# Folding the values of grouped heads into the first weights: eight 64x32 tiles per chunk in two banks instead of pairs of 128x64 tiles per half chunk

## The chip, the cores and the metric

The kernel runs on one core of a Trainium2 chip. The metric is the device time of one execution in microseconds (us); lower is better. A timing is the median of several runs.

## What is computed

Three stages follow each other. An attention over 32 memory slots per head reduces keys and values to 32 rows per head; a dense layer with a leaky activation and then a sum over four gated experts follow. Cut to what matters:

```python
# 4 batches, 8 heads, 576 tokens, head size 64, 32 memory slots
a = exp(phi - max(phi, axis=2)); a = a / (sum(a, axis=2) + 1e-9)
k_m = einsum('bhsm,bhsd->bhmd', a, k)
v_m = einsum('bhsm,bhsd->bhmd', a, v)
scores = q @ k_m.T / sqrt(64)
attn = softmax(scores)                       # 576 x 32 per head
x = concat_over_heads(attn @ v_m)            # 2304 x 512
h = x @ w_in                                 # w_in 512 x 2048
g = max(h, 0) + alpha * min(h, 0)
y = g @ w_out                                # w_out 2048 x 512
p = probs / (sum(probs) + 1e-9)
out = sum over e of p[:, e] * (max(y @ w1[e], 0) @ w2[e])   # 4 experts, 512 -> 1024 -> 512
```

## The kernel before

The product `attn @ v_m @ w_in` isn't formed in that order. For each batch b and each chunk c of 512 of the 2048 columns of `w_in`, the kernel first multiplies the 32 x 64 values of each head into the 64 rows of `w_in` that belong to that head. This is the **fold** (`fold`, line 519). Its result is a 256 x 512 matrix, 32 rows for each of the 8 heads, and the dense layer then multiplies it by the 256 x 576 attention weights of the batch.

A fold works on half a chunk (e is 0 or 1, 256 columns) and one PSUM bank. The 8 heads are two groups g of four. A stationary operand has 128 rows (two heads of 64) and 64 columns (2 x 32 memory slots), and is zero where the rows of one head meet the columns of the other. `att_sum` (line 285) makes these zeros with a small product by a mask (line 289), and `att_memc` (line 328) with two scaled copies that use it. There are four such matmuls of 256 columns in a fold, in float32, two for each group, side by side in the two halves of the array's columns. Then `fold_hi` (line 531, on ScalarE) copies the bank to SBUF in the rounded fp32r form, and `fold_lo` (line 536, on VectorE) writes the remainder. For batch 0, chunk 0 (`plain`) there is a float32 copy alone.

`First` is a step of the dense layer: chunk c, batch b, half k of the tokens (288 of them), and 128 columns f; there are 128 steps, numbered j = 32c + 8b + 4k + f. Its tasks are `u` (`up`: six fp32r matmuls on the folded weights, four float32 instructions where plain), `n` and `v` (the two sides of the activation, ScalarE and VectorE), `h` and `l` (rounded and remaining part, ScalarE and VectorE or GpSimd), `d` (`down`: 12 matmuls into four PSUM banks that stay open over four steps) and `e` (those four banks are emptied). The experts run after these steps.

All work is issued in an order written out by hand, the string `ORDER` (line 34), where `f`, `fh` and `fl` are the three tasks of a fold. In the kernel before their digits are batch, chunk and half; `f201` is batch 2, chunk 0, second half. Every engine works through its own instructions in that order. The names `a31_mem`, `a10_ev0` and so on are tasks of the attention of a batch and a group: `mem` is the product with keys and values, `memc` copies it out of PSUM, `sc0` and `sc1` are scores of the two halves of the tokens, `ev0` and `ev1` turn them out of PSUM on VectorE.

PSUM has eight banks. Two are kept for the `u` tasks. The other six (`ps_a`, line 208) are handed out to all else, in the order in which they came free: four are held by an open group of `d` tasks, and two are left for folds and for the attention. A task whose bank isn't free yet waits for the last reader of the bank that comes free next. Folded weights have four buffers (`wpp`, line 212).

The steps of the dense layer that need folds run from about 25 to 410 us, the experts after that.

Of the kernel before, what the change touches and what calls it, by code (L numbers as in the profile page):

```python
# [21 lines left out]
HB = S // 2  # L22
# [13 lines left out]
  a01_natc a01_nath a00_natc w2 a01_nathc a01_mem in0_1 in0_0 in0_2 a00_mem a01_memc in1_1 in1_0 out0_1 in1_2 a01_memt  # L36
  a00_memc in0_3 a01_memtc a00_memt out0_0 a01_sc0 a00_memtc in1_3 a00_sc0 a01_ev0 in0_4 w3 a00_ev0 q1 s010_max p2
  s000_max kv2 s010_sub a11_max s000_sub a10_max s010_exp a11_exp s010_sum in1_4 s000_exp a11_nat a10_exp s010_mul
  s000_sum f000 s010_back a11_natc s000_mul a10_nat a11_sum fh000 a11_nath s000_back a10_natc out0_2 u0 a11_nathc
  a01_sc1 out0_3 n0 a00_sc1 a01_ev1 out0_4 in2_1 u1 q2 a00_ev1 s01288_max in3_1 in2_0 a11_mem n1 s00288_max s01288_sub  # L40
  a10_sum s00288_sub s01288_exp in2_2 s00288_exp a10_mem a11_memc in3_0 out0_5 in3_2 a11_memt a10_memc in2_3 a11_memtc
  a10_memt s00288_sum in2_4 a11_sc1 a10_memtc s01288_sum a11_sc0 s00288_mul a10_sc1 a11_ev0 a10_sc0 v0 in3_3 s00288_back
  s01288_mul a10_ev1 in3_4 s01288_back d0
# [3 lines left out]
out2_5 out3_2 out3_3 u6 in5_1 out3_4 p3 v3 f100 out3_5 v4 n5 s100_max s110_sub d3  # L47
n6 a21_max v5 s110_exp s100_sub u7 e3 v6 out1_6 s110_sum f101 s100_exp a20_max out2_6 d4
fh100 s100_sum n7 s110_mul fl100 a21_exp d5
s100_mul a20_exp out3_6 s110_back fh101 s100_back d6  # L50
pst in6_1 s01288_lo fl101 s100_hi v7 s110_hi s100_lo d7
s110_lo a20_sum s00288_lo q3 a21_sum s000_lo u8 e7 s010_lo u9 in4_0 a20_nat in4_2 n8 a21_nat n9 u10 v8 in4_3 h8 a21_nath
  a21_natc u11 l8 v9 n10 d8
in5_0 a20_natc v10 a21_nathc in5_2 u12 h9 h10 a20_mem l9 l10 n11 in5_3 n12 v11 in6_0 a21_mem a20_memc v12 h11 in4_4
  a30_max h12 a30_exp l11 a20_memt kv3 l12 d9
a21_memc a30_sum in5_4 a20_memtc a31_max in7_1 a21_memt in6_2 a31_exp a20_sc0 u13 a20_ev0 a21_memtc a31_sum a20_sc1 n13
  in6_3 a21_sc1 out4_1 a20_ev1 in6_4 u14 a21_ev1 s200_max a21_sc0 n14 d10
s200_sub a21_ev0 s210_max a31_nat s210_sub s200_exp a30_nat v13 a31_natc d11
s200_sum s210_exp a30_natc s210_sum s200_mul a31_nath e11 f200 s210_mul u15 a31_nathc v14 d12
h13 s200_back h14 l13 s210_back fh200 l14 a31_mem n15 fl200 s200_hi v15 s210_hi s200_lo a30_mem a31_memc s210_lo h15  # L60
  in7_0 out5_1 l15 in7_2 a31_memt a30_memc u16 out4_0 a31_memtc u17 n16 out4_2 a30_memt n17 a31_sc0 v16 a30_memtc d13
v17 h16 a31_ev0 l16 in7_3 a30_sc1 h17 a30_sc0 l17 a30_ev1 a31_sc1 a30_ev0 in7_4 f201 s300_max a31_ev1 s300_sub d14
fh201 s310_max fl201 s300_exp d15
s310_sub out6_1 s300_sum s310_exp u18 e15 s310_sum s300_mul u19 f300 s310_mul n18 d16
s300_back n19 v18 s300_hi v19 u20 h18 s310_back s300_lo h19 d17
s310_hi l18 fh300 l19 u21 n20 s310_lo d18
n21 v20 fl300 h20 u22 l20 v21 d19
out4_3 h21 n22 l21 out4_4 u23 e19 v22 u24 out5_0 out6_0 f301 out5_2 h22 n23 d20
l22 fh301 v23 n24 fl301 d21
h23 v24 out4_5 l23 out5_3 h24 u25 l24 d22  # L70
n25 out4_6 out5_4 out7_1 v25 u26 out5_5 out6_2 h25 u27 n26 d23
l25 n27 v26 out6_3 h26 u28 e23 l26 u29 v27 out6_4 f010 out5_6 h27 n28 d24
l27 out7_0 n29 v28 d25
v29 h28 fh010 l28 out6_5 fl010 d26
h29 out7_2 in8_1 l29 u30 out7_3 d27
n30 out6_6 in9_1 v30 u31 out7_4 e27 in8_0 u32 in8_2 f011 h30 n31 l30 d28
in9_0 n32 v31 in9_2 h31 d29
fh011 l31 out7_5 v32 u33 out7_6 h32 d30
n33 l32 fl011 in10_1 v33 u34 in8_3 h33 d31
l33 n34 in9_3 v34 u35 e31 in10_0 u36 in10_2 f110 n36 in10_3 d32  # L80
h34 v36 fh110 l34 in8_4 n35 fl110 d33
h36 v35 in11_1 l36 u37 h35 in9_4 u38 l35 n37 in11_0 d34
n38 v37 in11_2 h37 out8_1 d35
l37 v38 out8_0 h38 u39 e35 in10_4 u40 n39 l38 f111 out9_1 v39 n40 d36
out8_2 h39 fh111 v40 d37
l39 h40 fl111 l40 u41 in11_3 d38
n41 out8_3 in11_4 v41 u42 out8_4 h41 d39
n42 l41 out9_0 out8_5 v42 u43 e39 out8_6 h42 u44 n43 l42 f210 out10_1 v43 n44 u45 out9_2 h43 d40
fh210 l43 v44 n45 fl210 d41
h44 v45 out11_1 l44 out9_3 d42  # L90
h45 l45 out10_0 u46 out9_4 out10_2 u47 n46 d43
n47 v46 out10_3 h46 out9_5 u48 l46 e43 u49 out9_6 n48 f211 v47 in12_1 v48 d44
h47 out11_0 fh211 l47 out10_4 fl211 d45
# [12 lines left out]
h60 fl020 out13_1 l60 u61 in15_2 d58
n61 out12_0 out12_2 u62 v61 d59
n62 in15_3 h61 v62 u63 l61 e59 h62 u64 l62 n63 f021 n64 v63 out12_3 h63 d60
fh021 l63 v64 fl021 in15_4 d61
h64 l64 out14_1 u65 out13_0 out12_4 d62  # L110
n65 out13_2 out12_5 u66 v65 out13_3 h65 u67 n66 l65 d63
out12_6 n67 v66 v67 h66 u68 e63 h67 l66 u69 out15_1 l67 n68 f120 out14_0 n69 v68 d64
out13_4 fh120 v69 out13_5 fl120 d65
h69 out14_2 d66
h68 l69 l68 out14_3 u70 out13_6 d67
out15_0 n70 out14_4 v70 out14_5 u71 e67 h70 out14_6 u72 n71 f121 l70 v71 n72 u73 out15_2 h71 d68
fh121 l71 fl121 n73 d69
# [6 lines left out]
h77 wl00 u78 e75 u79 n78 f221 l77 v78 n79 d76
ws01 h78 fh221 d77
fl221 u80 u81 f320 l78 v79 n80 d78
h79 v80 fh320 l79 u82 h80 fl320 n81 d79
l80 v81 n82 u83 e79 h81 u84 l81 f321 n83 v82 h82 d80
v83 fh321 l82 h83 fl321 n84 l83 u85 u86 v84 n85 d81
h84 v85 l84 n86 d82  # L130
h85 v86 l85 d83
h86 l86 u87 e83 u88 n87 f030 n88 v87 h87 d84
v88 fh030 l87 fl030 d85
h88 l88 d86
d87
u89 e87 u90 n89 f031 n90 v89 h89 d88
v90 fh031 l89 h90 fl031 u91 l90 u92 n91 d89
n92 v91 h91 v92 u93 l91 h92 u94 l92 n93 d90
n94 v93 h93 v94 d91
l93 h94 l94 u95 e91 u96 n95 f130 n96 v95 h95 d92  # L140
v96 fh130 l95 fl130 d93
h96 l96 u97 u98 n97 d94
n98 v97 h97 v98 u99 l97 h98 d95
l98 n99 v99 u100 e95 h99 u101 l99 n100 f131 n101 v100 d96
v101 fh131 fl131 d97
h100 l100 d98
h101 l101 u102 u103 n102 d99
n103 v102 h102 v103 u104 l102 e99 h103 u105 l103 n104 f230 n105 v104 d100
fh230 v105 fl230 d101
h105 l105 d102  # L150
h104 l104 u106 u107 n106 d103
n107 v106 h106 v107 u108 l106 h107 e103 u109 l107 n108 f231 n109 v108 d104
v109 fh231 x0t0 x0h0 fl231 d105
# [38 lines left out]
def memory_attention_experts(ctx: ExitStack, tc: tile.TileContext, phi, q, kv, w_in, w_out, w1, w2, alpha, dp, out):  # L192
# [42 lines left out]
    mask = const.tile([128, 2], F32, name="mask")  # L235
# [1125 lines left out]
```

## Time and profile before

| | |
|---|---|
| median of 3 runs | 1166.19 us (1165.74 to 1166.47) |
| span of the profiled execution, first to last instruction | 1164.3 us |
| TensorE (PE) busy, share of the span | 1142.6 us, 98% |
| VectorE (DVE) | 853.2 us, 73% |
| ScalarE (ACT) | 473.1 us, 41% |
| GpSimd (POOL) | 410.0 us, 35% |
| mean granted TensorE clock | 0.994 of 2.4 GHz |

The profile gives no time of the profiled execution beside its span; the median of the runs lies 1.9 us above the span. Busy time of TensorE is the time in which at least one matmul is under way, and matmuls overlap, so its cost is read from starts: from the start of one group of matmuls to the start of the next. PEld are the loads of stationary operands. A row of a timeline says start, length, engine, line, operation, what is written and read, shapes, count, and in brackets the idle time ahead of it and who ended it. One matmul call on float32 operands makes two instructions, and one on fp32r makes one.

### The profile page before, as it was taken

The page shows a single profiled execution, that of the slowest core. Times are in us where ns is not written, and L with a number is a line of the kernel's source. Part 1 is how long each engine was busy: PE and PEld are TensorE (multiplying, and loading weights), DVE is VectorE, ACT ScalarE, POOL GpSimd, SP SyncE. Part 2 cuts the span into 40 slices and gives each one's busy share as a digit, 9 for nine tenths or more (in the row PEclk, how much of TensorE's full clock was granted, in tenths as well). Part 3 has the DMA queues.
Part 4 walks back from the last instruction along what each step waited for, and adds up shares of the span by engine and source line. Part 5 has one row for each costly group of instructions (what it writes and reads, how often), then busy time and mean ns, then how long its engine had stood idle before and what let it go on. Part 6 is the DMA issues. An engine that isn't in the chain of part 4 may idle for free.

```text
span 1164.3 us, 21801 instructions
## 1 busy us (share of the span) xinstructions
PE 1142.6 (98%) x8628; PEld 1096.0 (94%) x8628; DVE 853.2 (73%) x1573; ACT 473.1 (41%) x1035; POOL 410.0 (35%) x333
## 2 busy tenths in 40 slices
PE   8899999999999989999999999999999999999998
PEld 7578999999999989999999999999999999999998
DVE  6999888885558674767757766678667777777794
ACT  5567756555455534333323333223432222222220
POOL 2333022322010164745646456433333333333320
PEclk9999999999999989999999999999999999999999
DMA  9740221312000262745637455485545556555512
GB/s 375 274 177 20 73 91 55 91 37 82 1 1 1 85 258 104 279 169 212 242 120 296 152 220 227 172 303 197 181 158 189 164 165 185 162 181 182 163 65 72
DMA packets 64214, 180.02 MB, mean 155 GB/s; under 512 B 6640, under 2 KB 23024, under 8 KB 60400
## 3 DMA queue, kind: packets, MB, share of 16 engines
q1 hardware_dynamic: 64112, 178.63, 43.9%
q8 instruction: 68, 1.11, 0.4%
q14 instruction: 34, 0.28, 0.1%
HBM read 114.34 MB, written 64.26 MB: 153 GB/s over the span
## 4 chain that ended last, share of the span: by engine, by line
PE 88%; DVE 7%; DMA 2%; issue 2%; POOL 1%; ACT 1%; SPq 0%; DVEq 0%; ACTq 0%; POOLq 0%
PE o L914 18%; PE y L600 17%; PE c L978 13%; PE uy L806 12%; PE h L562 8%; PE ux L806 8%; PE uw L806 8%; PE pw L523 2%; DMA rawin<-in_w_in 2%; DVE g L232 1%; PE pm L325 0%; POOL g L232 0%; POOL w L232 0%; DVE h L884 0%; DVE g L581 0%
## 5 line engine op out<-in xcount | busy, mean ns | idle before, releaser
L914 PE MATMUL o<-g,w 128*128 128x288 f32 x1536 | 226.0, 296 | 0.7 <-DVE g L232 0.4
L914 PEld LDWEIGHTS o<-g,w 128*128 128x128 f32 x1536 | 211.6, 189 | 1.1 <-DVE g L232 0.6
L600 PE MATMUL y<-g,wout 128*128 128x288 f32 x1440 | 205.5, 297 | 0.0
L600 PEld LDWEIGHTS y<-g,wout 128*128 128x128 f32 x1440 | 194.2, 188 | 10.5 <-issue 7.0
L806 PE MATMUL uy<-x,w 128*128 128x288 f32 x1152 | 186.0, 297 | 3.4 <-DVE v L840 3.4
L806 PEld LDWEIGHTS uy<-x,w 128*128 128x128 f32 x1152 | 163.9, 189 | 6.0 <-DVE v L840 5.9
L978 PE MATMUL c<-gc,w2c 128*128 128x288 f32 x1008 | 156.3, 295 | 0.5 <-ACT acc L991 0.5
L978 PEld LDWEIGHTS c<-gc,w2c 128*128 128x128 f32 x1008 | 141.1, 188 | 1.0 <-ACT acc L991 1.0
L232 POOL TENSOR_TENSOR gc<-h,gc 128x576 fp32r<-128x576 f32 x56 | 83.0, 1490 | 143.0 <-ACT gc L965 99.9
L806 PE MATMUL ux<-x,w 128*128 128x288 f32 x768 | 122.8, 295 | 2.8 <-ACT v L844 2.7
L806 PE MATMUL uw<-x,w 128*128 128x288 f32 x768 | 122.7, 295 | 0.0
L806 PEld LDWEIGHTS ux<-x,w 128*128 128x128 f32 x768 | 108.6, 188 | 3.2 <-ACT v L844 3.2
L965 ACT CAST gc<-h 128x576 fp32r<-128x576 f32 x70 | 47.3, 675 | 152.0 <-DVE h L957 138.6
L562 PE MATMUL h<-a,wp 128*128 128x288 f32 x720 | 108.8, 296 | 0.1
L806 PEld LDWEIGHTS uw<-x,w 128*128 128x128 f32 x768 | 108.8, 188 | 0.0
L232 POOL TENSOR_TENSOR w<-raww,w 128x512 fp32r<-128x512 f32 (+1 forms) x48 | 76.3, 1606 | 86.6 <-ACT w L705 59.8
L562 PEld LDWEIGHTS h<-a,wp 128*128 128x128 f32 x720 | 99.5, 188 | 2.7 <-issue 1.3
L931 DVE TENSOR_TENSOR acc<-o,acc 128x288 f32<-128x288 f32 x112 | 50.8, 454 | 69.2 <-PE o L914 69.2
L581 DVE SCALAR_TENSOR_TENSOR pos<-neg,nal,pos 128x288 f32<-128x288 f32 x120 | 64.8, 544 | 43.0 <-ACT pos L576 42.5
L840 DVE TENSOR_TENSOR v<-uy,v 128x288 f32<-128x288 f32 x128 | 58.1, 454 | 50.7 <-PE uy L806 50.6
L575 ACT ACTIVATE neg<-h 128x288 f32<-128x288 f32 x128 | 53.0, 414 | 83.3 <-PE h L562 78.6
L232 POOL TENSOR_TENSOR g<-pos,g 128x288 fp32r<-128x288 f32 x29 | 24.4, 845 | 173.0 <-ACT g L585 142.8
(163 smaller groups left out, 1670.9 us busy)
## 6 DMA issues: line engine op xcount, KB each, us to landing
kw<-w SPq DMA_DIRECT2D x16, 1792.0 KB, 6.9
raww<-in_w SPq DMA_DIRECT2D x32, 512.0 KB, 3.9
w<-kw SPq DMA_DIRECT2D x32, 512.0 KB, 4.6
kS<-S SPq DMA_DIRECT2D x56, 256.0 KB, 5.0
w2c<-kS SPq DMA_DIRECT2D x28, 512.0 KB, 3.6
kw<-w SPq DMA_DIRECT2D x25, 512.0 KB, 2.7
w<-kw SPq DMA_DIRECT2D x48, 256.0 KB, 3.9
kv<-in_kv SPq DMA_DIRECT2D x8, 1152.0 KB, 12.6
```

The lines of the kernel that those rows point to most:

```text
L232: eng.tensor_tensor(out=out, in0=in0, in1=in1.bitcast(F32), op=ALU.subtract)
L523: mm(p[64 * j:64 * j + 64, g * 256:(g + 1) * 256], vt_t[b, g][:, j, :], win_t[c][:, 2 * g + j, e * 256:(e + 1) * 256], start=True, stop=True,)
L562: mm(p, wp_t[b, c, f // 2][:, x, o2 + g * 256:o2 + g * 256 + 128], a_t[b][:, y, g, o:o + HB], start=(n == 0), stop=(n == 5))
L575: nc.scalar.activation(out=neg, in_=p, func=AF.Relu, scale=-1.0)
L581: nc.vector.scalar_tensor_tensor(out=pos, in0=neg, scalar=nal[:, ft:ft + 1], in1=pos, op0=ALU.mult, op1=ALU.add)
L600: mm(First.acc[d], w[:, x, d * 128:(d + 1) * 128], self.gt[:, y, 0:HB], start=(self.start and n == 0), stop=(self.stop and n == 2))
L806: mm(p, w[:, x, a, k], operand(self.b, i)[:, y, k], start=(start and n == 0), stop=(n == 5), skip_group_check=not start)
L840: nc.vector.tensor_tensor(out=out, in0=x, in1=y, op=ALU.add)
L914: mm(self.p, w[:, x, i, d % 2 * 128:(d % 2 + 1) * 128], g, start=(m == 0), stop=(m == 11), skip_group_check=len(hps) == 1)
L931: nc.vector.tensor_tensor(out=a, in0=self.p, in1=a, op=ALU.add)
L965: nc.scalar.copy(out=t[:, 0], in_=self.raw[q])
L978: mm(self.p, w[:, x, i, m * 128:(m + 1) * 128], self.g_t[q][:, y, i], start=(k == 0), stop=(k == 5))
```

## The change

Group u now holds the four heads of parity u (0, 2, 4, 6 or 1, 3, 5, 7); the host lays out `phi`, `k` and `v` to fit, and `q` stays as it was. `att_memc` writes the product twice side by side, in one instruction, with a scale for each row, so the mask and its product are gone. After the transposition, rows 0 to 63 and 64 to 127 of `kt` and `vt` both hold keys or values, and group u uses rows 64u to 64u + 63. Scores take four 64x32 tiles for each group and half instead of two of 128x64.

A fold takes a whole chunk: eight matmuls of 512 columns, one for each head, each on a 64x32 tile of the array (row half u, column quarter t), into two banks, one for each u. For batch 0, chunk 0 it takes half a chunk, eight matmuls of 256 columns, also into two banks. `fh` and `fl` then come once for each u. In `ORDER` the fold of a whole chunk and its `fh` and `fl` stand where those of the first half stood, and the places of the second half are empty. Nothing else in `ORDER` moves.

```diff
     def att_sum(b, g):
-        nc.vector.tensor_scalar(out=mr, in0=mask, scalar1=sm, scalar2=None, op0=ALU.mult)
     def att_memc(b, g):
-        for u in range(2):
-            nc.scalar.activation(
-                out=kvb[:, :, u, :],
-                in_=p[:, 0:128].rearrange("p (t d) -> p t d", t=2),
-                func=AF.Copy,
-                scale=stats[b, g][1][:, u:u + 1],
-            )
+        nc.scalar.activation(
+            out=kvb,
+            in_=p[:, 0:128].rearrange("p (t u d) -> p t u d", t=2, u=1).to_broadcast([128, 2, 2, D]),
+            func=AF.Copy,
+            scale=stats[b, g][0],
+        )
     def att_score(b, g, hf):
-        for j in range(2):
-            o = (hf * 4 + 2 * g + j) * HB
-            mm(p[64 * j:64 * j + 64, 0:HB], kt[:, j, :], q_t[b][:, o:o + HB], start=True, stop=True)
+        r = slice(64 * g, 64 * g + 64)
+        for t in range(4):
+            o = (hf * 4 + t) * HB
+            mm(p[32 * t:32 * t + 32, 0:HB], kt[r, 32 * t:32 * t + 32], q_t[b][r, o:o + HB], start=True, stop=True)
-    def fold(b, c, e):
-        p = pw_t[b, c, e] = bank(f"pw{b}{c}{e}")
-        for g in range(2):
-            for j in range(2):
+    def fold(b, c, cols):
+        n0, n1 = cols
+        for u in range(2):
+            pw_t[b, c, u, n0] = bank(f"pw{b}{c}{u}{n0}")
+        for t in range(4):
+            for u in range(2):
+                r = slice(64 * u, 64 * u + 64)
                 mm(
-                    p[64 * j:64 * j + 64, g * 256:(g + 1) * 256],
-                    vt_t[b, g][:, j, :],
-                    win_t[c][:, 2 * g + j, e * 256:(e + 1) * 256],
+                    pw_t[b, c, u, n0][32 * t:32 * t + 32, 0:n1 - n0],
+                    vt_t[b, u][r, 32 * t:32 * t + 32],
+                    win_t[c][r, t, n0:n1],
                     start=True,
                     stop=True,
                 )
```

A part of `ORDER`, where folds stood for batch 2 and chunk 0:

```diff
-s200_sum s210_exp a30_natc s210_sum s200_mul a31_nath e11 f200 s210_mul u15 a31_nathc v14 d12
-h13 s200_back h14 l13 s210_back fh200 l14 a31_mem n15 fl200 s200_hi v15 s210_hi s200_lo a30_mem a31_memc s210_lo h15
+s200_sum s210_exp a30_natc s210_sum s200_mul a31_nath e11 f20 s210_mul u15 a31_nathc v14 d12
+h13 s200_back h14 l13 s210_back fh200 fh201 l14 a31_mem n15 fl200 fl201 s200_hi v15 s210_hi s200_lo a30_mem a31_memc s210_lo h15
-v17 h16 a31_ev0 l16 in7_3 a30_sc1 h17 a30_sc0 l17 a30_ev1 a31_sc1 a30_ev0 in7_4 f201 s300_max a31_ev1 s300_sub d14
-fh201 s310_max fl201 s300_exp d15
+v17 h16 a31_ev0 l16 in7_3 a30_sc1 h17 a30_sc0 l17 a30_ev1 a31_sc1 a30_ev0 in7_4 s300_max a31_ev1 s300_sub d14
+s310_max s300_exp d15
```

And the part around the second fold of batch 0, chunk 0, of which only the `fh` changes:

```diff
-a11_ev1 out1_1 v1 out1_0 s000_hi f001 out1_2 s010_hi s00288_hi fh001 out1_3 s01288_hi u2 out1_4 out0_6 s110_max u3
-  out2_1 a10_ev0 n2 d1
+a11_ev1 out1_1 v1 out1_0 s000_hi f001 out1_2 s010_hi s00288_hi fh0010 fh0011 out1_3 s01288_hi u2 out1_4 out0_6 s110_max u3
+out2_1 a10_ev0 n2 d1
```

## Rows read from the trace of the kernel before

**Rows 1.** Windows by stage; an engine's columns are busy us and instructions
```profile
core 0: us, PE busy (x) PEld busy (x) DVE busy (x) ACT busy (x) POOL busy (x), PEclk, DMA share, GB/s
30.00:80.00 50.00, 43.33 (x326) 31.57 (x318) 48.53 (x88) 30.27 (x79) 17.48 (x15) 0.97 0.57 208
80.00:100.00 20.00, 19.57 (x199) 15.27 (x200) 19.27 (x42) 16.06 (x46) 5.53 (x5) 1.00 0.32 121
100.00:250.00 150.00, 149.90 (x1116) 138.68 (x1114) 129.29 (x257) 91.30 (x232) 31.64 (x29) 1.00 0.23 71
250.00:372.00 122.00, 122.00 (x909) 113.53 (x906) 77.97 (x157) 61.87 (x156) 15.61 (x18) 1.00 0.05 20
```

**Rows 2.** Groups of TensorE by form: count, busy us, mean ns, idle before
```profile
L523 PE MATMUL pw<-win,vt 128*64 128x256 f32 x256 | 34.6, 391 | 0.0
...
L357 PE MATMUL pc<-q,kt 128*64 128x288 f32 x64 | 10.7, 454 | 0.1
...
L325 PE MATMUL pm<-kv,pe 128*32 128x128 f32 x256 | 8.6, 276 | 0.0
```

**Rows 3.** Timeline of TensorE alone, a stretch with one fold, then without
```profile
118.24 1.76 PE L562 MATMUL h<-a,wp 128*128 128x288 f32 x12
119.93 1.08 PE L523 MATMUL pw<-win,vt 128*64 128x256 f32 x8
120.94 3.44 PE L600 MATMUL y<-g,wout 128*128 128x288 f32 x24
124.22 0.95 PE L562 MATMUL h<-a,wp 128*128 128x288 f32 x6
125.01 1.78 PE L600 MATMUL y<-g,wout 128*128 128x288 f32 x12
126.63 1.74 PE L562 MATMUL h<-a,wp 128*128 128x288 f32 x12
128.21 1.75 PE L600 MATMUL y<-g,wout 128*128 128x288 f32 x12
```

**Rows 4.** Timelines of TensorE in narrow windows inside one fold
```profile
102.42 0.60 PE L523 MATMUL pw<-win,vt 128*64 128x256 f32 x4
...
102.64 0.82 PE L523 MATMUL pw<-win,vt 128*64 128x256 f32 x6
...
103.07 0.39 PE L523 MATMUL pw<-win,vt 128*64 128x256 f32 x2
```

**Rows 5.** Groups by form in the first 120 us: mask product, scaled copies
```profile
L332 ACT ACTIVATE kvb<-pm,mr 128x128 f32<-128x128 f32 x16 | 4.9, 359 | 0.3
...
L289 DVE TENSOR_SCALAR mr<-mask,sm 128x2 f32<-128x2 f32 x8 | 2.1, 268 | 0.4
```

**Rows 6.** Timeline around the second fold of batch 0, chunk 0
```profile
40.96 1.08 PE L523 MATMUL pw<-win,vt 128*64 128x256 f32 x8
...
42.73 2.21 PE L559 MATMUL h<-pe,wp 128*128 128x288 f32 x8 [0.69 <-ACT wp L534]
...
44.13 0.47 DVE L362 STREAM_TRANSPOSE pe<-pc 128x288 f32<-128x288 f32 x1
44.15 0.68 ACT L463 ACTIVATE mout<-rawout 128x512 f32<-128x512 f32 x1 [1.14 <-DMA rawout<-in_w_out]
...
45.91 0.69 DVE L469 SCALAR_TENSOR_TENSOR mout<-mout,sout 128x512 uint32<-128x512 uint32 x1
...
49.88 2.21 PE L597 MATMUL y<-g,wholeout 128*128 128x288 f32 x8 [1.07 <-DVE wholeout L496]
```

**Rows 7.** Timeline where batch 3's products with keys and values start
```profile
93.10 0.65 DVE L232 TENSOR_TENSOR wp<-pw,wp 128x512 fp32r<-128x512 f32 x1
...
93.28 2.80 PE L325 MATMUL pm<-kv,pe 128*32 128x128 f32 x80
```

**Rows 8.** Timeline at the end of a group of d tasks
```profile
183.25 1.54 DVE L611 TENSOR_TENSOR y<-y,y 128x288 f32<-128x288 f32 x4
...
186.33 1.85 PE L600 MATMUL y<-g,wout 128*128 128x288 f32 x12
```

More of the change, by code (lines that the diff above doesn't have):

```diff
@@ L65 @@
+v17 h16 a31_ev0 l16 in7_3 a30_sc1 h17 a30_sc0 l17 a30_ev1 a31_sc1 a30_ev0 in7_4 s300_max a31_ev1 s300_sub d14
+s310_max s300_exp d15
+s310_sub out6_1 s300_sum s310_exp u18 e15 s310_sum s300_mul u19 f30 s310_mul n18 d16
 s300_back n19 v18 s300_hi v19 u20 h18 s310_back s300_lo h19 d17
[L66 to L69, printed above, removed]
+s310_hi l18 fh300 fh301 l19 u21 n20 s310_lo d18
@@ L123 @@
+v75 h74 out15_6 wopen h75 fh220 fh221 l74 d73
+l75 n76 fl220 fl221 n77 v76 d74
 h76 v77 wh00 l76 d75
[L124 to L129, printed above, removed]
+h77 wl00 u78 e75 u79 n78 l77 v78 n79 d76
+ws01 h78 d77
+u80 u81 f32 l78 v79 n80 d78
+h79 v80 fh320 fh321 l79 u82 h80 fl320 fl321 n81 d79
+l80 v81 n82 u83 e79 h81 u84 l81 n83 v82 h82 d80
@@ L529, in fold, with fold_hi, fold_lo @@
                 )
-    def fold_hi(b, c, e):
-        t = wp_t[b, c, e] = wpp.tile([128, 2, 512], F32R, tag="wp", name=f"wp{b}{c}{e}")
-        o = t[:, 0, :]
-        nc.scalar.copy(out=o.bitcast(F32) if plain(b, c) else o, in_=pw_t[b, c, e])
-    def fold_lo(b, c, e):
-        t, p = wp_t[b, c, e], pw_t[b, c, e]
+    def fold_hi(b, c, u, cols):
+        n0, n1 = cols
+        if (b, c, u) not in wp_t:
+            wp_t[b, c, u] = wpp.tile([128, 2, 512], F32R, tag="wp", name=f"wp{b}{c}{u}")
+        o = wp_t[b, c, u][:, 0, n0:n1]
+        nc.scalar.copy(out=o.bitcast(F32) if plain(b, c) else o, in_=pw_t[b, c, u, n0][:, 0:n1 - n0])
+    def fold_lo(b, c, u):
+        t, p = wp_t[b, c, u], pw_t[b, c, u, 0]
         sub_to(nc.vector, t[:, 1, :], p, t[:, 0, :])
@@ L561, in up @@
                 for x, y in PASSES:
[L562 removed]
+                    mm(p, wp_t[b, c, g][:, x, fs], a_t[b][:, y, g, o:o + HB], start=(n == 0), stop=(n == 5))
                     n += 1
@@ L1286, in memory_attention_experts @@
         for c in range(NC):
-            for e in range(2):
-                task(f"f{b}{c}{e}", fold, b, c, e)
-                task(f"fh{b}{c}{e}", fold_hi, b, c, e)
-                task(f"fl{b}{c}{e}", fold_lo, b, c, e)
+            if plain(b, c):
+                for e in range(2):
+                    cols = 256 * e, 256 * e + 256
+                    task(f"f{b}{c}{e}", fold, b, c, cols)
+                    for u in range(2):
+                        task(f"fh{b}{c}{e}{u}", fold_hi, b, c, u, cols)
+            else:
+                task(f"f{b}{c}", fold, b, c, (0, 512))
+                for u in range(2):
+                    task(f"fh{b}{c}{u}", fold_hi, b, c, u, (0, 512))
+                    task(f"fl{b}{c}{u}", fold_lo, b, c, u)
     task("q01", load_q, 0, 1)
@@ L1309, in memory_attention_experts @@
         make_identity(nc, ident)
-        nc.gpsimd.memset(mask, 0.0)
-        for h in range(4):
-            nc.gpsimd.memset(mask[32 * h:32 * h + 32, h % 2:h % 2 + 1], 1.0)
         for name in ORDER.split():
```

154 lines of the change are left out of this document (76 added, 78 removed).

## The prediction

> **What bounds the kernel now.** I read the table of windows first, since the change touches only the stretch from 23 to 370 us. From 100 to 372 us TensorE is busy 271.9 of 272 us at full granted clock, and VectorE 207.3 of 272 [rows 1]. Whatever TensorE is spared there, it can give to the end as long as nothing else takes over. From 80 to 100 us TensorE (19.57 of 20) and VectorE (19.27 of 20) are both nearly full, and from 30 to 80 us it is VectorE that is full (48.53 of 50) while TensorE stands idle for 6.7 us [rows 1]. So a fold before 80 us hides behind VectorE and is worth little, and one after 80 us is worth its whole price. In issue order the folds after 80 us are f200 and f201, f300 and f301 and the 24 of chunks 1 to 3: 28 half folds, 14 chunks. The experts behind them have no fold and come the earlier by what TensorE saves.
>
> **The price of a fold now.** The timeline of TensorE alone gives it by difference [rows 3]. From 118.24 to 124.22 us there are 36 matmuls of the dense layer and one fold, 5.98 us. From 124.22 to 128.21 us there are 30 such matmuls and no fold, 3.99 us or 0.133 each. So the fold costs 5.98 - 36 x 0.133 = 1.19 us. Inside there is a staircase [rows 4]: four instructions have started before 102.70, the first two of eight are over when the next begins at 102.64, and the last two start at 103.07. Two run side by side in each step, and the three steps take 0.65 us, 0.217 each for 256 columns. Streaming is thus 4 x 0.217 = 0.87 us. The other 0.32 us is the change from full tiles to half tiles and back.
>
> **The price of a fold after.** Eight calls of 512 columns are 16 instructions. If all eight tiles run side by side they make two steps, each of twice 0.217 = 0.434, again 0.87 us, for the whole chunk instead of half of it. To this I add 0.32 for entering and leaving the small tiles, and 0.05 for eight starts instead of two: 1.24 us. A chunk then costs 1.24 instead of 2.38, a gain of 1.14 us. No row shows two row halves at work at once, and this is what I don't know. Column tiles are shown: the products with keys and values use four tiles of 32 columns, and 80 instructions take 2.80 us [rows 7], of which the last instruction is 0.28 [rows 2]. That is 2.52/19 = 0.133 us for a step of four, and one after another they would be at least 80 x 0.108 (half of 0.217, for 128 columns) = 8.7 us. The bounds are therefore two steps (1.24 us) and, if the halves u = 0 and 1 take turns, four steps of 0.434, 2.06 us with the 0.32. I take the first, because streams in separate array tiles with separate banks resemble the four column tiles most. Sum: 14 x 1.14 = **16.0 us less**; at the other bound 14 x 0.32 = 4.5 us less.
>
> The Trainium skill has a sentence for each side. TensorE: Matmul & The Clock Gate, Part 3 (Packing small matmuls), reports that row and column tiles compose, 10.6 times for 16 tiles of 32x32; by it the first bound holds. TensorEngine Tiling (Array Packing), Key Properties, says that a change of tiling mode drains the engine; the 0.32 us above agree with that.
>
> **fh and fl.** There are as many as before, two copies and two differences of 128x512 for each chunk, only both in one place. Nothing of this is on TensorE, and the weights are needed about two steps later. The empty places behind give the time back. I count nothing; if VectorE fell behind it would be 0.6 us for one moved difference [rows 7].
>
> **Banks at a chunk's start.** Two banks are taken at once, so the first of the four new accumulators gets one that the preceding `e` has just emptied, where before it got an older one. The four emptying operations take 1.54 us from 183.25 and the new group starts at 186.33 [rows 8], so the first bank has been free for more than 2 us. Nothing is added.
>
> **f001 now waits.** Counting banks along the order: at f001 four are held by d0, one by the scores of `a10_ev0`, and one is left, but f001 now wants two. The second can only come from `a10_ev0`, which stands behind f001 in the order. VectorE does it at 44.13 to 44.60, and f001 began at 40.96 [rows 6], so TensorE waits some 3.6 us with u2, u3 and d1 behind it, and ScalarE waits at fh0010 with `out2_1` behind that. ScalarE did `out2_1` at 44.15, when its weights had come, and VectorE went on with it at 45.91 [rows 6]. Now ScalarE gets the fold at about 45.2 and does three copies first, so `out2_1` starts near 46.1 and VectorE goes on near 46.8: 0.8 us late in a stretch where it is the bound. On TensorE d2 comes near 51.3 instead of 49.88, where it had 1.07 us of waiting for VectorE to give [rows 6]. I take +0.8 and keep 0 to +3.6.
>
> **a31_mem now waits.** In the same count it finds no bank until fl200 has read its own. That difference ran from 93.10 to 93.75 and the product began at 93.28 [rows 7]: +0.5 us, in a stretch where TensorE is full. Bounds 0 and 1.2 (if it had to wait for fl201 as well).
>
> **Mask and copies.** Eight products of 0.268 us leave VectorE and eight of 16 copies of 0.359 leave ScalarE [rows 5], the remaining ones being twice as long in elements. Six of the products lie where VectorE is full: -1.1 to -1.6 us; I take -1.2, which about pays for the two waits. Most ScalarE time has cover.
>
> **Scores.** Four tiles of 32 columns instead of two of 64 in each task, the same streaming. Tasks are 16, in 10.7 us [rows 2], 0.67 each. Two neighbours with different row halves could overlap (-0.5 at three places), or the tiles could run in pairs (+0.5 for each of the seven tasks after 80 us). I take 0 and keep -1.5 to +3.5.
>
> The sum against the profiled span: 1164.3 - 16.0 + 0.8 + 0.5 - 1.2 = 1148.4. VectorE's load from 100 to 250 us rises from 86% to about 91%, and I allow 0.3 us for matmuls that meet it, 1148.7. The median is 1.9 us above the span: **1150.6 us**.
>
> **Rivals.** (a) The row halves take turns: 4.5 us instead of 16.0, which is **1162**. For it speaks that no row shows row tiles side by side; against it, that the column tiles do so without loss. (b) The end on the other side: the tiles of one row half run one after another, because a load of stationary values would have to wait for matmuls in its own rows. Each half then has 8 steps of 0.434, 3.47 us, both halves at once, so a chunk costs 3.79 instead of 2.38, 14 x 1.41 = 19.7 us more: **1186**. The point from which this decides is five steps of 0.434; from there a chunk costs as much as now. Against it speaks the step of 0.133 for four column tiles that share all their rows. The Trainium skill names this mechanism (TensorE: Matmul & The Clock Gate, Part 3, "What overlaps and what doesn't": loads overlap running matmuls only where the row groups differ); the rows of four column tiles speak against that rule here. (c) VectorE takes over: with 207.3 us of work against 272 - 16 = 256 it isn't full on the whole, but from 100 to 250 us waits in order could take half the gain: **1158**. Against it: TensorE stood idle 0.1 us in that whole stretch [rows 1]. (d) The waits for banks cost all of their 3.6 and 1.2 us: 1154, within the forecast's own range.
>
> **How the numbers follow.** The forecast has 0.76, its own range 1147.5 to 1154.5. (a) has 0.11, (b) 0.06, (c) 0.05, and 0.02 goes to something that eats the gain altogether. A measurement of this kernel can tell about 0.2% (2.3 us) from no change. Faster by more: the forecast, (c) and nearly all of (a), 0.91; same: 0.03; slower: (b), 0.06. The range runs from 1147.5, all scores overlapped, to 1162.5, so that (a) is in it.
>
> **What would show it.** The changed profile should have 16 instructions of 512 columns for each chunk (8 of 256 at a step for batch 0, chunk 0), whose starts form two bunches 0.43 us apart; a row of dense matmuls around a fold should come out at 1.24 us for the fold. Four bunches would mean (a), eight (b). TensorE should still be full from 100 to about 356 us; idle time there that VectorE ends would be (c). At 41 us a wait of TensorE for the line 362 of before should stand, and one of half a microsecond near 93 us. The forecast is wrong if a fold costs over 1.4 us, or if the stretch up to 80 us ends over 3 us later than now.

## The result

The changed kernel takes 1151.31 us (1150.61 to 1151.95) against 1166.33 us (1165.74 to 1166.64) for the kernel before: a ratio of 0.987 with a 95% interval of 0.9856 to 0.9884, or 15.0 us less. The forecast was 1150.6 us. Timed again beside three of the kernels below, it took 1151.1 us (1149.89 to 1151.9).

The windows of the changed kernel by stage answer to [rows 1]; the last ends at 356 us, since the folds now end that much earlier. An engine's columns are busy us and instructions.

```profile
core 0: us, PE busy (x) PEld busy (x) DVE busy (x) ACT busy (x) POOL busy (x), PEclk, DMA share, GB/s
30.00:80.00 50.00, 43.48 (x346) 31.16 (x339) 46.84 (x83) 29.53 (x75) 17.40 (x16) 0.86 0.53 196
80.00:100.00 20.00, 18.02 (x216) 13.82 (x214) 19.13 (x40) 15.74 (x42) 5.22 (x5) 1.00 0.38 148
100.00:250.00 150.00, 149.87 (x1190) 140.58 (x1188) 136.47 (x269) 96.23 (x246) 35.25 (x33) 1.00 0.24 71
250.00:356.00 106.00, 106.00 (x843) 99.99 (x841) 69.34 (x143) 56.91 (x144) 12.70 (x15) 1.00 0.06 23
```

From 100 us on TensorE is as full as it was, with VectorE at 136.47 of 150 us instead of 129.29 and not in the way. The new costs lie ahead of 100 us: TensorE's granted clock from 30 to 80 us is 0.86 instead of 0.97, and from 80 to 100 us TensorE is idle for almost 2 us.

The groups of TensorE by form answer to [rows 2] (count, busy us and mean ns, idle ahead and who ended it):

```profile
L523 PE MATMUL pw<-win,vt 64*32 64x512 f32 x240 | 16.3, 601 | 0.0
...
L354 PE MATMUL pc<-q,kt 64*32 64x288 f32 x128 | 7.8, 412 | 1.7 <-DMA q<-in_q 1.6
...
L523 PE MATMUL pw<-win,vt 64*32 64x256 f32 x32 | 2.8, 509 | 2.3 <-DVE pe L359 2.3
```

34.6 us of folds have become 16.3 + 2.8. The last column of the third row is one new wait.

The timeline of TensorE around a whole-chunk fold, and then the same fold in two narrow windows (131.43 to 131.80 and 132.05 to 132.30 us), answer to [rows 3, 4]. Columns are start, length, engine, line, operation and count.

```profile
128.09 1.75 PE L602 MATMUL y<-g,wout 128*128 128x288 f32 x12
129.68 1.76 PE L564 MATMUL h<-a,wp 128*128 128x288 f32 x12
131.37 1.09 PE L523 MATMUL pw<-win,vt 64*32 64x512 f32 x16
132.38 3.83 PE L602 MATMUL y<-g,wout 128*128 128x288 f32 x27
...
131.37 0.66 PE L523 MATMUL pw<-win,vt 64*32 64x512 f32 x8
...
131.82 0.64 PE L523 MATMUL pw<-win,vt 64*32 64x512 f32 x8
```

All eight tiles are under way from 131.37 on, and the second eight instructions (float32 makes two of each matmul) from 131.82: two bunches 0.45 us apart, not four and not eight. From the first start to the next dense matmul it is 1.01 us, for a whole chunk; half a chunk took the same 120.94 - 119.93 = 1.01 us before [rows 3]. A fold takes another 0.19 us that doesn't stand between these two starts: the 24 matmuls from 128.09 on would be over at 131.28 (24 x 0.133), and the fold starts 0.09 later; and the 24 matmuls behind a fold in [rows 3], from 120.94 to the next group at 124.22, take 0.10 us more than 24 x 0.1325, because the second of them starts that much late. So a fold costs 1.20 us, then as now, and a chunk costs one instead of two.

**Where the time went.** The table gives, for some tasks, the start in the kernel before and how much later (+) or earlier their first matmul starts in other kernels, worked out from the starts in the traces. "Again" is the second profile of the same kernel; the other columns belong to the experiments below.

| task | before, us | changed | changed, again | no wait at f001 | no wait at f001, again | early fl | row half 0 first, early fl | mask back |
|---|---|---|---|---|---|---|---|---|
| d0 | 37.16 | +0.37 | -0.15 | -0.23 | +0.23 | -0.11 | 0.00 | -0.08 |
| d2 | 49.88 | +4.24 | +4.16 | -0.55 | -0.08 | +3.93 | +1.13 | +3.94 |
| d9 | 77.48 | +1.45 | +1.05 | -1.14 | -0.67 | +1.08 | -0.53 | +1.12 |
| d10 | 85.19 | +0.80 | +0.22 | -1.75 | -1.36 | +0.47 | -1.15 | +3.01 |
| a31_mem | 93.28 | +1.98 | +0.77 | -1.20 | -0.19 | +0.48 | -1.13 | +4.09 |
| d14 | 103.38 | +1.11 | -0.09 | -2.06 | -1.05 | -0.18 | -1.85 | +3.23 |
| d20 | 120.94 | +0.01 | -1.19 | -3.16 | -2.16 | -1.28 | -2.95 | +2.14 |
| experts | 404.66 | -14.57 | -15.75 | -17.74 | -16.72 | -15.87 | -17.51 | -12.11 |
| end | 1164.33 | -14.17 | -16.24 | -17.26 | -16.39 | -14.91 | -17.43 | -11.53 |

From d20 to the experts lie the 12 chunks 1 to 3. They give 14.56 to 14.59 us in the first six of these columns (14.25 with the mask back), 1.21 for each chunk. Up to the experts, nearly all that differs between the columns arises ahead of d14. From the experts on the code is the same in all of them, and still the way from there to the end runs from 0.49 us shorter to 0.96 us longer than in the kernel before. The clock has a part in this: from 408 to 416 us TensorE's granted clock was 0.57 in the first profile of the changed kernel and 0.79 in the second. So a difference of a few tenths of a microsecond between medians below is not by itself the effect of an edit.

### The profile page after: what moved, and what is told of

Same layout as the page of the kernel before. It is cut to its first block, busy times and chain, and to the rows that moved or that the text cites. A ratio compares the mean times of both kernels' runs of the same rounds, so it can differ in the third digit from the quotient of the medians.

```text
span 1150.2 us, 21934 instructions
## 1 busy us (share of the span) xinstructions
PE 1125.5 (98%) x8708; PEld 1084.1 (94%) x8708; DVE 851.0 (74%) x1565; ACT 472.1 (41%) x1029; POOL 408.9 (36%) x328
## 3 DMA queue, kind: packets, MB, share of 16 engines
q8 instruction: 68, 1.11, 0.4%
## 4 chain that ended last, share of the span: by engine, by line
PE 87%; DVE 6%; DMA 2%; issue 2%; POOL 1%; ACT 1%; SPq 0%; DVEq 0%; ACTq 0%; POOLq 0%
PE o L916 18%; PE y L602 16%; PE c L980 13%; PE uy L808 12%; PE ux L808 8%; PE h L564 8%; PE uw L808 8%; PE pw L523 1%; DMA q<-in_q 1%; DMA rawout<-in_w_out 1%; DVE g L232 1%; PE h L561 1%; PE y L599 1%; POOL g L232 0%; POOL w L232 0%
## 5 line engine op out<-in xcount | busy, mean ns | idle before, releaser
L846 ACT COPY v<-ux 128x288 f32<-128x288 f32 x64 | 25.6, 401 | 144.5 <-PE ux L808 138.7
```

The costliest lines, as they stand in the source:

```text
L846: nc.scalar.copy(out=self.v1_t, in_=self.x)
```

## The experiments

Times are medians, and starts and waits come from one profiled execution of each run. Beside these kernels the kernel before took 1166.62 to 1166.9 us, beside the result 1166.33; each ratio goes by the one timed along with it. Three questions are open after the result: why a chunk costs what half of it did, what the waits for banks cost, and what the mask was worth.

**Cut by columns.** The 12 folds of chunks 1 to 3 in two parts, with the next `d` step between them (`f01x` behind `d24` and so on):

```diff
+        fold_part(b, c, n0, n0, n1 if plain(b, c) or not c else 256)
+
+    def fold_part(b, c, n0, m0, m1):
         for t in range(4):
             for u in range(2):
...
-                    pw_t[b, c, u, n0][32 * t:32 * t + 32, 0:n1 - n0],
+                    pw_t[b, c, u, n0][32 * t:32 * t + 32, m0 - n0:m1 - n0],
...
-                    win_t[c][r, t, n0:n1],
+                    win_t[c][r, t, m0:m1],
...
+                    task(f"f{b}{c}x", fold_part, b, c, 0, 256, 512)
```

> The changed kernel with the 12 folds of chunks 1 to 3 cut in two by columns: eight tiles of 256 columns, then the next d step, then eight tiles of the other 256 columns. Streaming is as before, but TensorE goes into small tiles and out again twice. Theory (0.32 us for going in and out, 0.05 for the eight starts): 12 x 0.37 = +4.4 us. Rival (going in and out costs nothing once the tiles overlap; the whole gain came from the row halves): 0, within 0.6 us.

Measured: 1157.16 us, a ratio of 0.9916 (0.9901 to 0.993) to the kernel before, and 5.9 us more than the changed kernel. The timeline of its TensorE around one of these folds:

```profile
131.95 0.66 PE L526 MATMUL pw<-win,vt 64*32 64x256 f32 x16
132.54 1.85 PE L605 MATMUL y<-g,wout 128*128 128x288 f32 x12
134.32 0.66 PE L526 MATMUL pw<-win,vt 64*32 64x256 f32 x16
134.92 2.25 PE L605 MATMUL y<-g,wout 128*128 128x288 f32 x15
```

Half the columns take 0.59 us between the two starts, and 0.78 with the 0.19 around it. Twice that is 1.56, 0.36 more than the 1.20 of the whole fold: the expected 12 x 0.36 = 4.4 us are there, and they are the way into small tiles and out again. The other 1.5 us are not folds: 0.6 us is lost ahead of d20, where the folds are as in the changed kernel, and the rest in single matmuls of the dense layer that come late, one of them 0.4 us late for VectorE. The rival, which has going in and out at nothing, falls.

**Cut by row half.** The same, with u = 0 in the first part and u = 1 in the second:

```diff
+        fold_part(b, c, n0, n1, (0,) if c else (0, 1))
+
+    def fold_part(b, c, n0, n1, us):
         for t in range(4):
-            for u in range(2):
+            for u in us:
...
+                    task(f"f{b}{c}x", fold_part, b, c, 0, 512, (1,))
```

> The changed kernel with the 12 folds of chunks 1 to 3 cut in two by row half: four tiles of u = 0 with 512 columns, then the next d step, then four tiles of u = 1. Each part is two steps of 0.434 us again, so the overlap of the row halves is lost, and TensorE goes in and out twice. Theory (row halves run at once in the changed kernel): 12 x (0.87 + 0.32) = +14.3 us, about 10 us more than the cut by columns. Rival (the row halves take turns anyway, and the gain comes from fewer changes of tile size): the same as the cut by columns, +4.4 us.

Measured: 1165.77 us (ratio 0.9993, 0.9984 to 1.0002): 14.5 us more than the changed kernel, and no different from the kernel before. The timeline of its TensorE at the same fold:

```profile
131.59 1.06 PE L526 MATMUL pw<-win,vt 64*32 64x512 f32 x8
132.58 1.85 PE L605 MATMUL y<-g,wout 128*128 128x288 f32 x12
134.36 1.06 PE L526 MATMUL pw<-win,vt 64*32 64x512 f32 x8
135.35 1.88 PE L605 MATMUL y<-g,wout 128*128 128x288 f32 x12
```

Four tiles of one row half take 0.99 us; eight of both took 1.01. So the second row half costs 0.02 us when it is issued along with the first. Of the 1.16 us that a chunk costs more here (2 x 0.99 + 2 x 0.19 against 1.20), 0.36 is the second way in and out by the cut above, and 0.80 the row half. The rival, by which this cut would have cost no more than the one by columns, falls by 8.6 us.

**Row half 0 first.** The order inside the fold, for all folds:

```diff
-        for t in range(4):
-            for u in range(2):
+        for u in range(2):
+            for t in range(4):
```

> The changed kernel with the two loops of the fold exchanged: the four tiles of row half 0 are issued first, then the four of row half 1, all in one fold. Theory (all eight tiles are under way within 50 ns, whatever their order): no change, within 0.6 us. Rival (a tile can only join while the one issued just before it works on other rows, so the order that alternates row halves is what lets them overlap): up to half of the overlap is lost, 14 x 0.87 = +12 us.

Measured: 1150.76 us (ratio 0.9863, 0.9848 to 0.9878), the same as the changed kernel. At the fold shown for the two cuts, its 16 instructions start at 130.34 and the next dense matmul at 131.36, 1.02 us again. So it doesn't matter whether the tile issued just before works on other rows. This kernel brought something that no theory had: its TensorE no longer waits 2.3 us for VectorE's line 359 at f001 (the third row of the groups above), but 0.50 us for ScalarE. A part of its timeline:

```profile
41.38 0.97 PE L523 MATMUL pw<-win,vt 64*32 64x256 f32 x8
...
42.43 0.37 ACT L536 COPY wp<-pw 128x256 f32<-128x256 f32 x1 [1.03 <-PE pw L523]
...
42.85 0.64 PE L523 MATMUL pw<-win,vt 64*32 64x256 f32 x8 [0.50 <-ACT wp L536]
```

With all of row half 0 ahead, `fh0010` can empty the first bank while row half 1 has none yet, and row half 1 then gets that bank after 0.50 us. With the halves interleaved both banks are needed at once. That the time is the same although this wait is gone has a reason in the profile: up to d7 this kernel was 0.48 us ahead of the kernel before, then its granted clock was 0.50 from 66.0 to 69.4 us, and d8 came 1.19 us late.

**The pairs of the kernel before, side by side.** The kernel before, in which the two half folds of each chunk of 1 to 3 come one behind the other; one of the 12 places:

```diff
-l25 n27 v26 out6_3 h26 u28 e23 l26 u29 v27 out6_4 f010 out5_6 h27 n28 d24
+l25 n27 v26 out6_3 h26 u28 e23 l26 u29 v27 out6_4 f010 f011 out5_6 h27 n28 d24
```

> The kernel before with the two half folds of each chunk issued one behind the other for chunks 1 to 3, an edit of ORDER alone: the same 128x64 tiles and the same streaming, but one way in and out of small tiles instead of two. Theory (mode change 0.32 us of each fold's 1.19): 12 x 0.32 = -3.9 us against the kernel before. Rivals: the whole gain of the change comes from doing a chunk in one place, -14 us; or nothing of it does, 0.

Measured: 1163.06 us (ratio 0.997, 0.9957 to 0.9982), 3.6 us less than the kernel before. Its TensorE:

```profile
131.87 1.95 PE L523 MATMUL pw<-win,vt 128*64 128x256 f32 x16
133.75 3.48 PE L600 MATMUL y<-g,wout 128*128 128x288 f32 x24
```

A chunk takes 1.88 us between the starts, 2.07 in all, against 2.40 for two separate folds: 0.33 for one way in and out. Both rivals fall. Doing a chunk in one place is worth a quarter of the gain, and three quarters are the row halves side by side.

**No wait for a bank at f001.** `a10_ev0`, which frees the second bank, is issued ahead of f001:

```diff
-a11_ev1 out1_1 v1 out1_0 s000_hi f001 out1_2 s010_hi s00288_hi fh0010 fh0011 out1_3 s01288_hi u2 out1_4 out0_6 s110_max u3
-out2_1 a10_ev0 n2 d1
+a11_ev1 out1_1 v1 out1_0 s000_hi a10_ev0 f001 out1_2 s010_hi s00288_hi fh0010 fh0011 out1_3 s01288_hi u2 out1_4 out0_6 s110_max u3
+out2_1 n2 d1
```

> The changed kernel with the task a10_ev0 issued ahead of f001 instead of behind d1, so that a bank comes free before f001 asks for its second one. Theory (the wait for a bank at f001 costs time): the wait of TensorE for line 359 of 2.3 us goes, and the span falls by 0.8 to 1.4 us, since d10 to d12 started 0.80 us late and u24 1.12 us late against the kernel before; the stretch at the lower granted clock, 36.2 to 49.8 us, gets shorter again. Rival (VectorE sets that stretch and hides the wait): no change, within 0.3 us.

Measured: 1151.05 us (1148.83 to 1151.85), ratio 0.9867 (0.9851 to 0.9884). The profiled execution agreed with the theory and went beyond it (d10 2.55 us earlier than in the changed kernel), while the median lay within 0.3 us of it, as the rival has it. So both were run again.

> The changed kernel as it is, on the same chip as the next three, so that differences of one or two microseconds can be read. Expected: 1151 to 1152 us, and a stretch at the lower granted clock of about 13 us from 36 us on in the profile. If that stretch is shorter here, it is no fixed property of the kernel, and the part of a gain that goes with it is not to be counted.

> a10_ev0 ahead of f001 once more. Its first profile showed 3.4 us at the lower clock and d10 2.55 us earlier than in the changed kernel, but the other three executions were 2.2 to 3.0 us longer, at a mean clock of 0.991 to 0.993. Theory (the wait costs time, apart from the clock): at least 0.8 us below the changed kernel in the medians. Rival (only the clock differs, and VectorE hides the wait): within 0.3 us.

Measured: 1151.1 us for the changed kernel, and 1150.1 us (1148.83 to 1150.81) without the wait, 1.0 us less; over both runs of each the difference of the medians is 0.6 us. The profiles (columns again) have d10 at +0.22 with the wait and at -1.36 without. So up to d10 the wait costs 1.6 to 2.5 us in the profiled executions, the clock included. The medians differ by 0.3 us in the first comparison and by 1.0 in the second; executions spread over up to 3 us and overlap, so the medians alone don't settle it (the kernel with row half 0 first and early fh and fl, below, bears the wait out). A part of that spread is the clock, below: the changed kernel's stretch at the lower clock was 13.6 us long in the first profile, and in the second two pieces of 3.4 and 6.8 us.

**Early fh and fl of f20.** The two banks of the fold are read before `a31_mem` asks for one:

```diff
-s200_sum s210_exp a30_natc s210_sum s200_mul a31_nath e11 f20 s210_mul u15 a31_nathc v14 d12
-h13 s200_back h14 l13 s210_back fh200 fh201 l14 a31_mem n15 fl200 fl201 s200_hi v15 s210_hi s200_lo a30_mem a31_memc s210_lo h15
+s200_sum s210_exp a30_natc s210_sum s200_mul a31_nath e11 f20 s210_mul fh200 fh201 u15 a31_nathc v14 fl200 fl201 d12
+h13 s200_back h14 l13 s210_back l14 a31_mem n15 s200_hi v15 s210_hi s200_lo a30_mem a31_memc s210_lo h15
```

> The changed kernel with fh200 and fh201 issued right behind s210_mul, and fl200 and fl201 behind v14, so that both banks of fold f20 are read long before a31_mem asks for one. Theory (a31_mem's wait for the bank costs time on a full TensorE): the wait of 1.11 us for line 232 goes and the end comes 1.1 us earlier. Rival (what TensorE waits for there is passed on, and the group behind it waits for VectorE instead): no change, within 0.3 us.

Measured: 1150.59 us (ratio 0.9861, 0.9846 to 0.9876), 0.5 to 0.7 us below the changed kernel, with executions that overlap. In the profile the wait is gone: from d10 to a31_mem nothing is lost (+0.47 to +0.48), where the changed kernel lost 1.18 us in one profile and 0.55 in the other. From d10 to d14 as a whole the changed kernel loses 0.31 us and gains 0.31 in its two profiles, and this one gains 0.65: by the profiles the wait costs 0.3 to 1.0 us.

**Both.** The two moves in `ORDER` together, twice.

> Both moves in ORDER together: a10_ev0 ahead of f001, and the copies and differences of f20 earlier. Theory (the two waits are apart, each costs its own time): the gains add, 1.9 to 2.5 us below the changed kernel, about 1149 us. Rival (one stretch hides what the other gives back): no more than the larger of the two gains, 1.1 to 1.4 us.

> Both moves in ORDER once more: 1.9 to 2.5 us below the changed kernel by the theory that each wait costs its own time, 1.0 to 1.4 us if only that of a31_mem does.

Measured: 1149.2 us (ratio 0.9852, 0.9837 to 0.9867), 2.1 us below the changed kernel as by the theory, and in the second run 1150.06 us (1148.17 to 1150.31) beside the changed kernel's 1151.1, 1.0 us below it as by the rival. All executions of both runs have a median of 1149.6, 1.7 us below that of the changed kernel's, between the two. So both moves together gain, but that the gains add in full isn't shown. In the second profile a stretch at the lower clock, from 64.9 to 68.3 us, took a part away.

**Row half 0 first, and early fh and fl.**

```diff
-        for t in range(4):
-            for u in range(2):
+        for u in range(2):
+            for t in range(4):
...
-s200_sum s210_exp a30_natc s210_sum s200_mul a31_nath e11 f20 s210_mul u15 a31_nathc v14 d12
+s200_sum s210_exp a30_natc s210_sum s200_mul a31_nath e11 f20 s210_mul fh200 fh201 u15 a31_nathc v14 fl200 fl201 d12
...
```

> The copies and differences of f20 earlier, and the loops of the fold exchanged (row half 0 first). With the loops exchanged f001 did not wait for a10_ev0: the second bank it took was the one that fh0010 had just emptied, after 0.50 us. Theory (the way in which the second bank is got doesn't matter, only that the wait for VectorE is gone): the same as both moves together within 0.6 us. Rival (f001's wait was hidden by VectorE anyway): the same as the earlier copies alone, 1.0 to 1.4 us below the changed kernel.

Measured: 1148.69 us (1148.18 to 1149.61), ratio 0.9847 (0.9834 to 0.9861): the fastest of all, 2.4 us below the changed kernel in the same comparison, and every execution of it was faster than any of that one's. Its TensorE is full from 80 to 100 us again:

```profile
80.00:100.00 20.00, 20.00 (x241) 15.19 (x243) 19.37 (x41) 15.88 (x42) 5.17 (x5) 1.00 0.28 110
```

The rival, a wait at f001 that VectorE hides, would have left it at 1.0 to 1.4 us. That the way in which the second bank is got doesn't matter isn't shown to 0.6 us: beside it, both moves together stood at 1150.06, 1.4 us higher.

**The mask product put back**, unused, on the changed kernel:

```diff
+    mask = const.tile([128, 2], F32, name="mask")
...
+        mr = stat.tile([128, 2], F32, tag="mr", name=f"mr{b}{g}")
+        nc.vector.tensor_scalar(out=mr, in0=mask, scalar1=sm, scalar2=None, op0=ALU.mult)
...
+        nc.gpsimd.memset(mask, 1.0)
```

> The changed kernel plus a mask product as the kernel before had it, eight small VectorE operations of about 0.27 us whose result nobody reads. Theory (six of the eight lie where VectorE sets the pace): +0.6 to +1.6 us. Rival (VectorE has slack at those places, the waits for banks being later): no change, within 0.3 us.

Measured: 1153.49 us (ratio 0.9886, 0.9872 to 0.9901), 2.2 to 2.4 us more than the changed kernel and above both expectations. Not where they put it: up to d9 at 77 us, with six of the eight products done, nothing is lost (+1.12, against +1.45 and +1.05). The loss comes behind that, and rows of its TensorE and its windows show it:

```profile
81.84 0.44 PE L341 MATMUL pt<-ident,kvb 128*128 128x128 f32 x2 [1.38 <-ACT kvb L331]
...
78.00:83.80 5.80, 4.42 (x45) 3.13 (x38) 5.45 (x12) 3.96 (x12) 1.10 (x1) 1.00 0.78 247
83.80:90.60 6.80, 6.62 (x41) 4.43 (x41) 5.07 (x12) 2.80 (x8) 2.43 (x2) 0.50 0.74 293
```

TensorE waits 1.38 us for the scaled copy, 0.5 to 0.7 longer than the changed kernel in its two profiles (0.87 and 0.69), and then its granted clock falls to 0.50 (1.2 GHz) for 6.8 us in which it is nearly full. Half of 6.8 us is 3.4, and 3.0 us are lost between d9 and a31_mem, where the changed kernel loses 0.5 us in one profile and gains 0.3 in the other. So in this execution, by estimate, the small products cost 0.5 to 0.7 us by themselves, and the rest hangs on the clock. Its other executions, 1152.55 to 1153.66 us, have no profile.

## Why the prediction came out as it did

The forecast of 1150.6 was 0.7 us below the result, inside its own range of 1147.5 to 1154.5. The mechanism was right, the closeness is in part luck, as the sum at the end of this section shows. By its steps:

- **The price of a fold.** 1.19 before, 1.20 measured; 1.24 predicted for a chunk after, 1.20 measured. The gain of 1.14 per chunk was 1.21 in chunks 1 to 3. The first of its two bounds held: row halves run side by side. Its split (0.87 of streaming, 0.32 for the mode, 0.05 for more starts) stands as well: the two cuts and the pairs give 0.33 to 0.36 us for one way in and out.
- **Rivals (a) and (b)**, row halves in turns and tiles of one row half one after another, fall: there are two bunches, 1.20 us and not 2.06 or 3.79. The Trainium skill says (TensorE: Matmul & The Clock Gate, Part 3, Packing small matmuls) that row and column tiles compose; the trace agrees, with 1.01 us for eight tiles beside 0.99 for four. The Trainium skill also says (TensorE: Matmul & The Clock Gate, Part 3, "What overlaps and what doesn't") that loads overlap running matmuls only where the row groups differ, which is (b). This doesn't hold here: with row half 0 first, four tiles that share their rows start 7 ns apart and are under way in the first bunch along with the other four.
- **Rival (c)**, VectorE takes over, falls: from 100 to 250 us TensorE is idle 0.13 us. So the two terms put at nothing there, `fh` and `fl` in one place and the banks at a chunk's start, were nothing.
- **The two chunks ahead of 121 us.** The step put every fold at 1.14. From d14 to d20, where f301 is gone, it is 1.10; from a31_mem to d14, where f201 is gone, it is 0.86 or 0.87 (0.66 to 0.72 with the early fl, where the third score waits 0.26 to 0.32 us for VectorE). The timeline of TensorE there in the kernel before, where the scores stood ahead of the fold of [rows 4], and then in the changed kernel:

```profile
100.59 2.00 PE L357 MATMUL pc<-q,kt 128*64 128x288 f32 x12
...
103.38 2.90 PE L600 MATMUL y<-g,wout 128*128 128x288 f32 x20
```

```profile
102.58 1.99 PE L354 MATMUL pc<-q,kt 64*32 64x288 f32 x24
104.50 1.72 PE L602 MATMUL y<-g,wout 128*128 128x288 f32 x11
```

  Three scores take 104.50 - 102.58 = 1.92 us until the dense layer goes on. Before, scores and fold took 103.38 - 100.59 = 2.79 together. The difference of 0.87 is 4 x 0.217, the streaming of the fold alone. Scores are small tiles too, so f201 paid no way in and out of its own there, and taking it away saved none of it. I had priced a fold by one among dense matmuls.
- **f001's wait.** The mechanism was right: TensorE waits 2.33 us for line 359 in the first profile and 3.3 in the second. The size was too small for the profiles: +0.8 was put in, 1.6 to 2.5 us are lost by d10 there, while the medians differ by 0.3 to 1.0. The rows that answer to [rows 6], from the timeline of the changed kernel:

```profile
41.65 1.06 PE L523 MATMUL pw<-win,vt 64*32 64x256 f32 x2
...
44.51 0.47 DVE L359 STREAM_TRANSPOSE pe<-pc 128x288 f32<-128x288 f32 x1
...
45.04 1.10 PE L523 MATMUL pw<-win,vt 64*32 64x256 f32 x14 [2.33 <-DVE pe L359]
46.21 0.65 ACT L536 COPY wp<-pw 128x256 f32<-128x256 f32 x2 [4.91 <-PE pw L523]
46.64 3.77 PE L561 MATMUL h<-pe,wp 128*128 128x288 f32 x8 [0.50 <-ACT wp L536]
47.08 0.68 ACT L460 ACTIVATE mout<-rawout 128x512 f32<-128x512 f32 x1
47.79 0.69 DVE L466 SCALAR_TENSOR_TENSOR mout<-mout,sout 128x512 uint32<-128x512 uint32 x1 [1.61 <-ACT mout L460]
```

  The chain is the one predicted (VectorE frees the bank, ScalarE copies the fold, does `out2_1`, and VectorE goes on with it), but VectorE goes on at 47.79 and not at 46.8, and d2 comes at 54.1 and not at 51.3. The prediction reckoned with full speed: the two `u` tasks, 2.21 us at 42.73 before [rows 6], now take 3.77. Much of it is given back up to d9, because VectorE sets the pace there.
- **a31_mem's wait** for fl200: from d10 on 1.18 and 0.55 us are lost in the two profiles; predicted 0.5 with bounds 0 and 1.2. By d14 it has cost 0.3 to 1.0. Its rows in the two, which answer to [rows 7]:

```profile
95.26 2.80 PE L322 MATMUL pm<-kv,pe 128*32 128x128 f32 x80 [1.11 <-DVE wp L232]
...
94.05 2.80 PE L322 MATMUL pm<-kv,pe 128*32 128x128 f32 x80 [0.46 <-DVE wp L232]
```

- **Mask.** Predicted -1.2 in places where VectorE is full. The step failed in its reason: with the products back, nothing was lost up to 77 us, and yet the median rose by 2.2 to 2.4 us; in the profiled execution the loss came behind 77 us. VectorE being full from 30 to 80 us [rows 1] doesn't mean that each 0.27 us taken from it comes off the path. The test has a limit: in the kernel that it was made on, f001's wait decides when d2 to d9 start, and it may have hidden a loss ahead of it. The changed kernel without f001's wait has d10 at -1.4 and -1.75 for all that the change does ahead of it; scores, copies and mask share that, and which has how much stays open.
- **Scores.** Predicted 0 with a lower bound of -1.5: TensorE's busy time for them went from 10.7 to 7.8 us, since neighbours of different row halves overlap. Two such neighbours took 1.12 us until the dense layer went on before (from 82.45 to 83.57) and take 0.76 now (from 83.62 to 84.38); from 80 to 86 us the scores were worth 0.4 us.

So the folds gave 14.57 + 1.10 + 0.87 = 16.5 us in the first profile, against 16.0 predicted. All else was put at +0.4 (0.8 + 0.5 - 1.2 + 0.3) and came to 16.54 - 14.17 = +2.4 there, of which 1.98 were lost by a31_mem and 0.40 behind the start of the experts. In the second profile it came to +0.3: 0.77 by a31_mem, and 0.49 given back in the experts. The folds gave 0.5 us more than forecast and all else cost up to 2.0 us more, so in the first profile errors of opposite signs cancel in part, and in the second there is little to cancel. The terms that were off are the waits and the mask ahead of 100 us, and the experts, which were put at no change.

## What to carry to other kernels

Small matmuls should be issued together until their tiles fill the array: eight 64x32 tiles took the time of four, and each separate visit to small tiles among dense matmuls cost a third of a microsecond, whatever was done in it (in the one place where other small tiles stood beside it, it cost none). When an operation is merged or moved ahead, count the buffers that it now needs at once and find who frees the last one; an order in which the first part can finish and hand its buffer on takes that wait away. Where an engine looks full in a window, don't price each of its operations at its length: put one back and see.

## What the runs showed of the hardware that was not expected

**The granted clock differs from execution to execution of one kernel.** Windows of three profiles of the first 50 us (the changed kernel, the same again, and without f001's wait):

```profile
43.40:50.00 6.60, 4.46 (x21) 2.68 (x22) 4.88 (x8) 2.58 (x7) 1.16 (x1) 0.51 0.26 88
...
40.00:43.40 3.40, 1.20 (x5) 0.33 (x3) 3.19 (x7) 1.11 (x4) 0.05 (x1) 1.00 0.78 319
43.40:50.00 6.60, 4.98 (x22) 3.05 (x23) 4.88 (x9) 2.81 (x7) 1.16 (x1) 0.50 0.29 84
...
43.40:50.00 6.60, 5.57 (x24) 4.07 (x23) 6.32 (x10) 4.83 (x11) 2.89 (x2) 1.00 0.54 154
```

In all three TensorE had been idle for 3.4 us ahead of d0 at 37 us, and the clock was at 1.2 GHz for some time from about 36.5 us on. Where f001 waits again, the clock is low until 50 us, in the second profile after it had come back in between; in the third, where it doesn't wait, it is at 2.4 GHz from 40 us on. The other profiles of the changed kernel and its variants agree on the first half alone: in the six with the wait the clock is low until 49.7 to 50.6 us, in the six without it the low stretch ends anywhere from 39.9 to 47.1 us. And idle time doesn't settle it: ahead of d7, at about 65 us, both kernels of the next two rows had 1.87 us of it. The first (both moves, the second profile) ran on at the lower clock, the other (without f001's wait) at the full one:

```profile
64.64 3.90 PE L599 MATMUL y<-g,wholeout 128*128 128x288 f32 x8 [1.87 <-DVE g L583]
...
64.64 2.21 PE L599 MATMUL y<-g,wholeout 128*128 128x288 f32 x8 [1.87 <-DVE g L583]
```

The eight matmuls take 3.90 us instead of 2.21, and 1.69 us is what such a stretch of 3.4 us costs where TensorE is the bound: that kernel's next `d` step goes from -1.14 to +0.55 against the kernel before, and nothing gives it back. Of the four profiles with 1.87 or 1.88 us of idle time there, the clock fell in two (the other is row half 0 first) and stayed up in two, so taking f001's wait away can bring a loss of this size with it. What decides whether the clock falls there was not found.

**The second dense matmul behind small tiles comes 0.10 us late**, in both kernels and behind every fold, besides the 0.09 us ahead of the first tile. Together with what lies inside the fold this is the 0.33 to 0.36 us for a way in and out. The Trainium skill says (TensorEngine Tiling (Array Packing), Key Properties) that a change of tiling mode drains the engine; the two gaps agree with that, and the price doesn't depend on how many tiles or columns follow.
